# An attention and MoE kernel on one core: the fourth pair of the first group gets raw buffers of its own, GpSimd may round weights, VectorE no longer divides or copies for the early pairs

## Chip, cores, metric

One Trainium2 chip, one core. Times are device microseconds of that core for one execution of the whole program; smaller is better.

## What is computed

The reference is attention with a local window and a few global keys, and behind it a feed-forward layer (called MoE in the code; there is one expert):

```python
batch, n_heads, seq, head_dim = (4, 8, 768, 64)      # n_global 8, n_local 96
scores = scale * np.matmul(q, k.transpose(0, 1, 3, 2))
bias = -slopes[:, None, None] * dist[None, :, :]     # dist: |i - j|, n_local for global keys
scores = np.where(keep, scores + bias, -1000000000.0)
a = np.exp(scores - np.max(scores, axis=-1, keepdims=True))
a = a / (np.sum(a, axis=-1, keepdims=True) + 1e-09)
x = np.matmul(a, v)                                  # to [3072 tokens, 512]
h = x @ w_in                                         # 512 x 2048
g = np.where(h > 0.0, h, np.exp(np.minimum(h, 0.0)) - 1.0)
out = g @ w_out                                      # 2048 x 512
```

The weights come in as 64-bit floats and are turned into pairs of rounded 32-bit floats on the chip.

## The kernel before

**Tiling.** Tokens go in 12 groups of 256 (four batches, three groups each). Attention of a group is done in four pairs of heads, numbered hp 0 to 3; each pair has two tiles of 128 queries for two heads. A tile sees 232 keys (96 before it, 8 global ones, 128 of its own); the first tile of a batch sees 128. The two weight matrices are cut into 16 chunks of 128 hidden columns, fc 0 to 15. The first three groups go chunk by chunk (fc 0 to 4 for each of the three groups, then 5 to 9, then 10 to 15) with weights that are prepared meanwhile; from the fourth group on the MoE runs in a denser form (`moe7`), one fixed order for all groups.

**A pair of an early group** (`pair` and `pair32`, L482 and L677). Two loads bring it in: `rqv` (queries and values, L516, or L507 and L498 for the first three pairs) and `rk` (keys, L517 or L501). The queries are scaled (L528). TensorE makes the scores `s` (L691), VectorE adds the bias table and takes the maximum (`softmax`, L647), ScalarE takes the exponential with its sum (L649), VectorE adds 1e-9 and inverts the sums (L662, L663), and the four tiles `pr` are multiplied by the inverse: the division (`norm`, L671; helper `scaled`, L633 on ScalarE, L635 on VectorE, L637 on GpSimd). TensorE transposes (`t`, L708), the transposes are copied out of PSUM (`pt`, L715 and L718), TensorE multiplies with the values (`pv`, L725), and the result is rounded into `xh` (L533) with its remainder (L534). The helper `copy` is L336 on ScalarE and L338 on VectorE or GpSimd; `minus` is L344.

**A weight** (`weight`, L413). One load of 512 KB (`bits`, L425), then ScalarE's absolute value (L433), four steps of VectorE (L434, L438, L440, L442), the rounding to the high half (L444, run as L336) and the subtraction for the low half (L445, run as L344).

**The order.** The program is straight-line code, written in the order that a planner finds. Every operation is added with `p.add(alts, emit, reads, writes, due, ...)`. `alts` lists the engines that may do it, each with a planned duration and a mark for using the port that VectorE and GpSimd share (helpers `act`, `dve`, `pool`, L260 to L269). The planner takes operations as their inputs and buffers come free, by due time, and gives one with several engines to the engine on which it would end first. Each engine then runs its own list in order. All of these loads are issued by SyncE (SP) but one; its list is in order too, so a load that waits for a buffer holds up the loads behind it. Loads of early weights have the due time of their chunk less 9000: 21000 and 24500 for the first layer's chunks 0 and 1, 26800 and 30300 for the second layer's. Loads of raw pairs are due at the pair's time less 9000; for the fourth pair of the first group this is 11000.

**Buffers.** A tile class has named slots. Raw pairs of the first three groups have three slots each: `rqv0`, `w015`, `w115` for `rqv` and `rk0`, `w014`, `w114` for `rk` (the last two are weights' places that are not in use yet). `ks0` and `qs0` belong to later groups.

**After planning** (`run`, L1044) the loads of the chunks in `ASKED` (2, 3 and 4, both layers) are moved up in the list, to stand right behind the second group's second pair's load (`self.loads[10]`).

Of the kernel before, what the change touches and what calls it, by code (L numbers as in the profile page):

```python
# [16 lines left out]
P = 128  # L17
# [4 lines left out]
HK = WN // 2  # L22
NT = 2
W = NT * P
BIG = float(2 ** 100)

HI, LO = 0, 1
# [238 lines left out]


def pool(n, two=True):
    return (("POOL", (30 + 2.58 * n) if two else (50 + 1.1 * n), True),)  # L269


def sp():
# [3 lines left out]
class Kernel:  # L276
# [136 lines left out]
    def weight(self, which, fc, due, after):  # L413
# [21 lines left out]
        else:  # L435
# [5 lines left out]
              [bits, g], [g], due - 4500)  # L441
        p.add(dve(DM, port=True), lambda e: nc.vector.scalar_tensor_tensor(g.t, low(), 29, g.t, ALU.logical_shift_right, ALU.bitwise_or),  # L442
              [bits, g], [g], due - 4000)
        p.add(act(DM), lambda e: self.copy(e, w.t[:, HI], gf()), [g], [w], due - 3000)  # L444
        p.add((pool(DM) if due < 90000.0 else ()) + dve(DM, port=True), lambda e: self.minus(e, w.t[:, LO], gf(), w.t[:, HI]),  # L445
              [g, w], [w], due - 2000)
        if which == 0 or fc < self.NF7:
# [34 lines left out]
    def pair(self, b, gi, hp, xh, xl, due, ahead, step, X):  # L482
# [8 lines left out]
        rv = rqv if rows else self.sb("rv", "rv", [P, VC])  # L491
        rk = self.sb("rk", "rk", [P, nk], slots=X.get("rk"))
        src = self.qkv[b, gi, hp]
        early = due - 9000 if rows else ahead - 9000
        if b == gi == 0 and hp < 3:

            vs, ks = slice(nq + P, nq + VC), slice(k0, nk)
# [26 lines left out]
        if rows:  # L524

            if "held" in X:
                self.loads += loads
            p.add((() if b == gi == 0 and hp < 3 else act(W) + dve(W, True)) + pool(W, False),  # L528
                  lambda e: self.scaled(e, q32(), q32(), sc), [rqv], [rqv], due - 9000)
            pv = self.bank("pv", "pv", [P, NT, P], X.get("pv"))  # L530
            self.pair32(b, hp, t0, q32, k32, v32, rqv, rk, pv, due, step, X)
            pvs = lambda: pv.t.rearrange("p i w -> p (i w)")
            p.add(act(W, True) + dve(W), lambda e: self.copy(e, xh.t[:, HI, hp], pvs()), [pv], [xh], due + 700)  # L533
            p.add(dve(W), lambda e: self.minus(e, xh.t[:, LO, hp], pvs(), xh.t[:, HI, hp]), [pv, xh], [xl], due + 800)  # L534
            if "held" in X:
                self.held += [o for v in (rqv, rk) for o in v.readers]
            return
# [132 lines left out]

    def norm(self, pr, lo, st, i, due, both):  # L671
        n = WN - lo
        more = act(n, extra=90) + pool(n, False) if both else act(n)
        self.plan.add(more + (("DVE", 130 + 0.53 * n, True),), lambda e: self.scaled(
            e, pr.t[:, lo:], pr.t[:, lo:], st.t[:, 2, i:i + 1]), [pr, st], [pr], due)

    def pair32(self, b, hp, t0, q32, k32, v32, rqv, rk, pv, due, step, X):  # L677
# [22 lines left out]
        for j in range(2):  # L700
            for i, x in enumerate(tiles):
                self.norm(prs[j][i], x[2], st, j * NT + i, d - 3000 + 2 * j + i, True)
            tp = self.bank("t", "t", [P, NT, 2, P], X.get("t"))

            def transposes(e, j=j, tp=tp):
                for i, (_, _, _, a0, kr, blocks) in enumerate(tiles):
                    for a in range(a0, 2):
                        nc.tensor.transpose(tp.t[:kr, i, a], prs[j][i].t[:, blocks[a]], self.ident.t)  # L708

            n = sum(2 - x[3] for x in tiles)  # L710
            p.add((("PE", 20 + 108.0 * n, False),), transposes, prs[j], [tp], d - 2500 + j)
            pt = self.sb("pt", "pt", [P, NT, 2, P], slots=X.get("pt"))
            pts.append(pt)
            if t0:
                p.add(act(NT * 2 * P, True) + dve(NT * 2 * P), lambda e, pt=pt, tp=tp: self.copy(e, pt.t[:HK], tp.t[:HK]), [tp], [pt], d - 2000 + j)  # L715
            else:
                for i, (_, _, _, a0, kr, _) in enumerate(tiles):
                    p.add(act((2 - a0) * P, True) + dve((2 - a0) * P), lambda e, pt=pt, tp=tp, i=i, a0=a0, kr=kr: self.copy(  # L718
                        e, pt.t[:kr, i, a0:], tp.t[:kr, i, a0:]), [tp], [pt], d - 2000 + j)

        def values(e):
# [213 lines left out]
    def build(self):  # L935
# [25 lines left out]
        for n, (b, gi) in enumerate(groups):  # L961
            lo, hi = (0.0, self.T0) if n == 0 else (start[n - 1], start[n])
            lead = self.LEAD[n >= self.LATER]
            lo -= lead[0] if n else 0.0
            hi -= lead[1] if n else 0.0
            lo, hi = self.ATT.get(n, (lo, hi))
            st = (hi - lo) / (4 * self.NP)
            for hp in range(self.NP):
                d = lo + (hp + 1) * (hi - lo) / self.NP
                X_ = self.EARLY[min(n, len(self.EARLY) - 1)]  # L970
                if n > self.GS:
                    X_ = {"seven": True}
                ahead = last - 2500
                if n > self.GS:
                    ahead = start[self.GS] + self.PERIOD * (4 * (n - self.GS - 1) + hp - 2) + self.VISIT
                    d, st = ahead + self.AFTER, 600.0
                todo.append((d if X_.get("rows") else max(self.ATT[self.GS][1] + 1, last + 1 - 2 * self.PERIOD), lambda b=b, gi=gi, hp=hp, n=n, d=d, st=st, X_=X_, ahead=ahead: self.pair(
                    b, gi, hp, *X[n], d, ahead, st, X_)))
                last = d
# [36 lines left out]
    AFTER = 2 * PERIOD  # L1016
    PASSES, SINCE = 2, 195000.0
    GS, KEEP, COMBO = 3, 100000.0, 0.0
    LATE, ASKED = 11, (2, 3, 4)
    ABS = (0, 1)  # L1020
    LINE = 32
    PLACE = {"w015": (80, 0), "w014": (0, 48), "w012": (80, 0), "w013": (0, 48), "xh0": (160, 0), "xh1": (32, 0), "gg0": (80, 0), "gg1": (0, 0)}
# [293 lines left out]
```

## Time and profile before

| what | value |
|---|---|
| time, median of 3 runs | 654.95 us (654.11 to 655.26) |
| the profiled execution | 655.49 us, its span 653.7 us |
| TensorE busy | 642.0 us (98% of the span) |
| VectorE busy | 522.0 us (80%) |
| ScalarE busy | 478.4 us (73%) |
| GpSimd busy | 27.1 us (4%) |

The span runs from the first to the last instruction; the time has a little more around it. TensorE's records are pipelined and overlap, so that it can look busy while it is not at its full pace; the share of its weight loads (PEld) tells more. Shares over the whole span are a mean over stages: the tables by stage tell them apart.

### The profile page before, as it was taken

What the parts mean: (1) busy time and instruction counts of PE and PEld (TensorE: products, weight loads), DVE (VectorE), ACT (ScalarE), POOL (GpSimd) and SP (SyncE); (2) the same over time, 40 slices, a digit from 0 to 9 for tenths busy, and PEclk for the clock granted to TensorE, in tenths of its full rate; (3) what the DMA queues carried; (4) which work ended last, traced back from release to release, by engine and by line L of the source; (5) the groups of instructions that cost most, each with busy time, mean ns of one, the idle gap of its engine ahead of it and who ended that gap; (6) DMA issues with size and microseconds to landing.
All of it is one profiled execution on the core that took longest, in us unless ns stands there. A gap on an engine that the chain in (4) does not pass through costs nothing.

```text
span 653.7 us, 15985 instructions
## 1 busy us (share of the span) xinstructions
PE 642.0 (98%) x5950; PEld 599.4 (92%) x5950; DVE 522.0 (80%) x1520; ACT 478.4 (73%) x1244; POOL 27.1 (4%) x54
## 2 busy tenths in 40 slices
PE   8899999999999999999999999999999999999996
PEld 6677888888888999999999999999999999999996
DVE  7999999999999867866877886876777778766655
ACT  6898888765778777776777777776777777774442
POOL 3152100000000000000000000000000000000000
PEclk9999999999999999999999999999999999999999
DMA  8835996810237567667756756766775675574661
GB/s 273 293 118 193 383 379 223 301 61 17 71 114 255 198 212 255 224 196 224 264 187 214 272 180 221 253 218 202 230 262 181 223 282 189 178 255 169 209 211 36
DMA packets 52373, 137.71 MB, mean 211 GB/s; under 512 B 5698, under 2 KB 19010, under 8 KB 52290
## 3 DMA queue, kind: packets, MB, share of 16 engines
q1 hardware_dynamic: 52000, 136.37, 61.6%
q8 instruction: 48, 0.79, 0.5%
q14 instruction: 35, 0.29, 0.1%
q10 hardware_dynamic: 290, 0.26, 0.1%
HBM read 119.84 MB, written 16.78 MB: 209 GB/s over the span
## 4 chain that ended last, share of the span: by engine, by line
PE 90%; DVE 4%; ACT 2%; DMA 2%; issue 1%; POOL 0%; DVEq 0%; POOLq 0%; SPq 0%
PE h L803 39%; PE a L880 26%; PE o L763 9%; PE pv L614 4%; PE s L556 3%; PE t L576 3%; PE s L691 2%; DMA rqv<-in_qkv_dram 2%; PE pv L725 2%; PE t L708 2%; ACT pr L649 1%; DVE g L464 1%; PE none L1084 0%; DVE gl L344 0%; ACT pt L336 0%
## 5 line engine op out<-in xcount | busy, mean ns | idle before, releaser
L803 PE MATMUL h<-xh,w0s 128*128 128x256 f32 x1728 | 203.1, 276 | 0.0
L803 PEld LDWEIGHTS h<-xh,w0s 128*128 128x128 f32 x1728 | 199.5, 188 | 0.1
L880 PE MATMUL a<-w,gg 128*128 128x256 f32 x864 | 143.7, 277 | 0.3 <-DVE xh L344 0.3
L336 ACT CAST gg<-z 128x384 fp32r<-128x384 f32 (+1 forms) x144 | 81.4, 566 | 69.7 <-DVE z L735 29.7
L735 DVE SCALAR_TENSOR_TENSOR z<-z,h 128x512 f32<-128x512 f32 x72 | 49.5, 688 | 92.9 <-ACT z L734 86.0
L880 PEld LDWEIGHTS a<-w,gg 128*128 128x128 f32 x864 | 120.4, 188 | 0.6 <-DVE xh L344 0.5
L649 ACT ACTIVATE pr<-pr,nmax 128x232 f32<-128x232 f32 (+1 forms) x192 | 90.0, 471 | 9.2 <-DVE nmax L647 8.9
L344 DVE TENSOR_TENSOR gg<-z,gg 128x512 fp32r<-128x512 f32 (+1 forms) x144 | 84.9, 618 | 7.2 <-ACT gg L336 6.6
L803 PEld LDWEIGHTS h<-xh,w 128*128 128x128 f32 x576 | 81.7, 188 | 8.8 <-issue 1.1
L803 PE MATMUL h<-xh,w 128*128 128x256 f32 x576 | 86.7, 282 | 0.1
L835 DVE TENSOR_TENSOR z<-z 128x128 f32<-128x128 f32 (+1 forms) x216 | 72.0, 333 | 5.2
L880 PE MATMUL a<-ta,gg 128*128 128x256 f32 x432 | 72.2, 276 | 0.0
L647 DVE CUSTOM_DVE_ANT_0 pr<-s,tab 128x232 f32<-128x232 f32 (+1 forms) x192 | 63.5, 374 | 5.6 <-PE s L556 5.6
L733 ACT ACTIVATE z<-h 128x512 f32<-128x512 f32 x72 | 43.0, 597 | 33.2 <-PE h L803 32.9
L763 PE MATMUL o<-w,gh 128*128 128x512 f32 x192 | 59.8, 403 | 0.8 <-ACT gh L336 0.4
L880 PEld LDWEIGHTS a<-ta,gg 128*128 128x128 f32 x432 | 59.6, 188 | 0.0
L880 PE MATMUL a<-tb,gg 128*128 128x256 f32 x216 | 50.0, 294 | 0.0
L734 ACT ACTIVATE z<-z 128x512 f32<-128x512 f32 x72 | 45.5, 632 | 1.8
L633 ACT ACTIVATE pr<-pr,st 128x232 f32<-128x232 f32 (+1 forms) x90 | 38.9, 469 | 9.6 <-DVE st L669 7.3
L880 PEld LDWEIGHTS a<-tb,gg 128*128 128x128 f32 x216 | 34.4, 188 | 3.8 <-issue 0.2
L763 PEld LDWEIGHTS o<-w,gh 128*128 128x128 f32 x192 | 31.8, 188 | 5.8 <-ACT gh L336 1.1
L649 ACT ACTIVATION_READ_ACCUMULATOR pr<-pr,nmax 128x1 f32 x192 | 36.8, 192 | 0.0
(126 smaller groups left out, 916.4 us busy)
## 6 DMA issues: line engine op xcount, KB each, us to landing
w0s<-kept SPq DMA_DIRECT2D x144, 512.0 KB, 5.0
rk<-in_qkv_dram SPq DMA_DIRECT2D x45, 184.0 KB, 2.8
bits<-in_w_in_dram SPq DMA_DIRECT2D x16, 512.0 KB, 6.5
bits<-in_w_out_dram SPq DMA_DIRECT2D x16, 512.0 KB, 9.4
kept<-w SPq DMA_DIRECT2D x16, 512.0 KB, 4.4
rv<-in_qkv_dram SPq DMA_DIRECT2D x32, 256.0 KB, 3.6
rqv<-in_qkv_dram SPq DMA_DIRECT2D x13, 384.0 KB, 3.5
rqv<-in_qkv_dram SPq DMA_DIRECT2D x34, 128.0 KB, 3.8
```

What stands on the lines that cost most here:

```text
L336: self.nc.scalar.copy(out, x)
L344: self.on(e).tensor_tensor(out, x, y, ALU.subtract)
L633: self.nc.scalar.activation(out, x, AF.Copy, scale=sc)
L647: p.add((("DVE", 158 + 1.042 * n, False),), lambda e: nc.vector.tensor_tensor_reduce(pr.t[:, lo:], st_()[:, lo:], tab, -(2.0 ** -(h + 1)), ...
L649: p.add(act(n, extra=200), lambda e: nc.scalar.activation(pr.t[:, lo:], pr.t[:, lo:], AF.Exp, bias=nm, scale=-1.0, accum_out=st.t[:, 0, i: ...
L733: p.add(act(n, True), lambda e: nc.scalar.activation(out(), hx(), AF.Relu, scale=-1.0), [h], [ex], due)
L734: p.add(act(n), lambda e: nc.scalar.activation(out(), out(), AF.Exp, scale=-1.0), [ex], [ex], due)
L735: p.add(dve(n), lambda e: nc.vector.scalar_tensor_tensor(out(), out(), -1.0, hx(), ALU.add, ALU.max), [h, ex], [ex], due)
L763: nc.tensor.matmul(acc[i].t, g.t[:, i * P:(i + 1) * P], w2.t[:, s], start=fc == f0 and n == 0 and s == HI, stop=fc == f1 - 1 and n == 1)
L803: self.nc.tensor.matmul(hx(), w1.t[:, s, cc * P:(cc + 1) * P], xh.t[:, x, cc], start=n == 0 and cc == 0, stop=n == 2 and cc == self.NCC - 1)
L835: tt = lambda e, out, x, y, op: self.on(e).tensor_tensor(out, x, y, op)
L880: nc.tensor.matmul(of[i].t[:, j], gg.t[:, x, g], w(s), start=first and x == s == 0 and (n in (0, 2, 4, 6) or final and n == 5), stop=last ...
```

## The change

- The class of planned durations for GpSimd: one-input work is planned at 30 + 1.85 ns a column instead of 50 + 1.1 ns, and no longer marked as using the shared port. A new entry `cast` plans a rounding on GpSimd at 50 + 1.14 ns a column.
- The rounding of a weight's high half may run on ScalarE or GpSimd (before: ScalarE).
- The scaling of queries, the division of early pairs, the copies of transposes and the rounding of attention output lose VectorE as an alternative. Divisions and scalings stay with ScalarE or GpSimd, the two kinds that read PSUM with ScalarE.
- The fourth pair of the first group takes `ks0` for `rqv` and `qs0` for `rk`, and its loads are due at 25000 instead of 11000.
- `ASKED` holds chunk 2 alone.

```diff
 def pool(n, two=True):
-    return (("POOL", (30 + 2.58 * n) if two else (50 + 1.1 * n), True),)
+    return (("POOL", (30 + 2.58 * n) if two else (30 + 1.85 * n), two),)
+
+
+def cast(n):
+    return (("POOL", 50 + 1.14 * n, False),)
...
-        p.add(act(DM), lambda e: self.copy(e, w.t[:, HI], gf()), [g], [w], due - 3000)
+        p.add(act(DM) + cast(DM), lambda e: self.copy(e, w.t[:, HI], gf()), [g], [w], due - 3000)
...
-        early = due - 9000 if rows else ahead - 9000
+        early = X.get("asked", due - 9000) if rows else ahead - 9000
...
-            p.add((() if b == gi == 0 and hp < 3 else act(W) + dve(W, True)) + pool(W, False),
+            p.add((() if b == gi == 0 and hp < 3 else act(W)) + pool(W, False),
                   lambda e: self.scaled(e, q32(), q32(), sc), [rqv], [rqv], due - 9000)
...
-            p.add(act(W, True) + dve(W), lambda e: self.copy(e, xh.t[:, HI, hp], pvs()), [pv], [xh], due + 700)
+            p.add(act(W, True), lambda e: self.copy(e, xh.t[:, HI, hp], pvs()), [pv], [xh], due + 700)
...
-        more = act(n, extra=90) + pool(n, False) if both else act(n)
-        self.plan.add(more + (("DVE", 130 + 0.53 * n, True),), lambda e: self.scaled(
+        more = act(n, extra=90) + pool(n, False) if both else act(n) + (("DVE", 130 + 0.53 * n, True),)
+        self.plan.add(more, lambda e: self.scaled(
...
-                p.add(act(NT * 2 * P, True) + dve(NT * 2 * P), lambda e, pt=pt, tp=tp: self.copy(e, pt.t[:HK], tp.t[:HK]), [tp], [pt], d - 2000 + j)
+                p.add(act(NT * 2 * P, True), lambda e, pt=pt, tp=tp: self.copy(e, pt.t[:HK], tp.t[:HK]), [tp], [pt], d - 2000 + j)
...
-                    p.add(act((2 - a0) * P, True) + dve((2 - a0) * P), lambda e, pt=pt, tp=tp, i=i, a0=a0, kr=kr: self.copy(
+                    p.add(act((2 - a0) * P, True), lambda e, pt=pt, tp=tp, i=i, a0=a0, kr=kr: self.copy(
...
+                if n == 0 and hp == 3:
+                    X_ = dict(X_, rqv=["ks0"], rk=["qs0"], asked=25000.0)
...
-    LATE, ASKED = 11, (2, 3, 4)
+    LATE, ASKED = 11, (2,)
```

## Rows read from the trace of the kernel before

**Rows 1.** Engines by stage: stretch, its length, busy us (instructions) of PE, PEld, DVE, ACT, POOL, then clock, DMA.

```profile
5.00:60.00 55.00, 50.81 (x392) 38.76 (x389) 51.99 (x186) 48.82 (x156) 16.71 (x26) 1.00 0.63 213
60.00:201.00 141.00, 140.35 (x991) 122.33 (x992) 137.53 (x374) 108.74 (x297) 7.95 (x16) 1.00 0.55 200
```

**Rows 2.** The chain that ended last, 0 to 70 us: start, length, what.

```profile
19.52 4.09 DMA rqv<-in_qkv_dram
...
23.63 0.51 ACT rqv L633
...
34.02 0.73 PE o L763 x2
...
46.73 3.60 DMA rqv<-in_qkv_dram
...
59.28 0.60 POOL pr L637
```

**Rows 3.** TensorE in order of time: start, length, engine, line, operation, tiles, shape, count.

```profile
17.31 0.89 PE L691 MATMUL s<-rk,rqv 64*128 64x128 f32 x8
...
26.87 1.07 PE L803 MATMUL h<-xh,w 128*128 128x256 f32 x4
```

**Rows 4.** Loads: SyncE's issues in time; issue to landing and rates, 5.5 to 26 us.

```profile
5.08 0.43 SPq L425 DMA_DIRECT2D bits<-in_w_in_dram  x1
...
13.01 0.33 SPq L516 DMA_DIRECT2D rqv<-in_qkv_dram  x1
...
GB/s 349 403 422 346 342 318 330 384 440 392 416 416 442 367 370 376 322 214 327 180 24 0 0 90 156 414 154 175 155 131 137 398 344 344 308 200 224 296 376 360
...
bits<-in_w_in_dram SPq DMA_DIRECT2D x4, 512.0 KB, 5.7
rqv<-in_qkv_dram SPq DMA_DIRECT2D x3, 384.0 KB, 3.4
```

**Rows 5.** VectorE's groups, 5 to 60 us: count, busy us, mean ns, idle before.

```profile
L635 DVE TENSOR_SCALAR pr<-pr,st 128x232 f32<-128x232 f32 x8 | 3.0, 392 | 0.0
L635 DVE TENSOR_SCALAR rqv<-rqv,scale 128x256 f32<-128x256 f32 x5 | 2.5, 503 | 0.3 <-DMA rqv<-in_qkv_dram 0.3
...
L338 DVE CAST xh<-pv 128x256 fp32r<-128x256 f32 x3 | 1.2, 405 | 0.0
L338 DVE COPY pt<-t 116x256 f32<-116x256 f32 x2 | 0.8, 425 | 0.2 <-ACT pt L336 0.2
L338 DVE COPY pt<-t 116x512 f32<-116x512 f32 x1 | 0.7, 676 | 0.0
```

**Rows 6.** ScalarE's groups, 5 to 60 us, and one row of its timeline.

```profile
L336 ACT CAST w<-g 128x512 fp32r<-128x512 f32 x9 | 5.6, 618 | 0.0
...
L633 ACT ACTIVATE pr<-pr,st 128x232 f32<-128x232 f32 x11 | 5.2, 489 | 1.2 <-DVE st L663 1.2
...
L336 ACT COPY pt<-t 116x256 f32<-116x256 f32 x6 | 2.2, 373 | 0.0
...
L633 ACT ACTIVATE rqv<-rqv,scale 128x256 f32<-128x256 f32 x3 | 1.5, 509 | 1.0 <-DMA rqv<-in_qkv_dram 1.0
...
28.63 0.68 ACT L433 ACTIVATE g<-bits 128x512 f32<-128x512 f32 x1
```

**Rows 7.** GpSimd: a row of its timeline, and two groups of 5 to 60 us.

```profile
9.03 0.80 POOL L637 TENSOR_SCALAR pr<-pr,st 128x128 f32<-128x128 f32 x2 [2.60 <-ACT pr L649]
...
L344 POOL TENSOR_TENSOR w<-g,w 128x512 fp32r<-128x512 f32 x4 | 5.2, 1296 | 3.2 <-ACT w L336 3.0
...
L637 POOL TENSOR_SCALAR rqv<-rqv,scale 128x256 f32<-128x256 f32 x1 | 0.5, 481 | 1.0 <-DMA rqv<-in_qkv_dram 1.0
```

**Rows 8.** VectorE and GpSimd at the same time, from their timelines.

```profile
12.18 1.44 POOL L637 TENSOR_SCALAR pr<-pr,st 128x128 f32<-128x128 f32 x2 [2.35 <-DVE st L663]
...
52.75 1.27 POOL L344 TENSOR_TENSOR w<-g,w 128x512 fp32r<-128x512 f32 x1 [0.62 <-ACT w L336]
...
52.78 1.52 DVE L344 TENSOR_TENSOR gl<-e,gh 128x256 fp32r<-128x256 f32 x1
```

## Prediction

> **What bounds the kernel now.** I read the table of engines by stage first [rows 1]. From 60 to 201 us TensorE is busy 140.35 of 141 us, and its weight loads fill 122.33 us, 87% of the stage: the matmuls follow each other without a hole, so no other engine's work costs time there, and the steady part behind it goes on in the same way. From 5 to 60 us it is different. The weight loads fill only 38.76 of 55 us (70%). At the later stage's density that much loading would need 38.76 / 0.868 = 44.7 us, so 10.3 us are holes, and more in truth, because warm-up matmuls on the tile `none` count as work here. In that stage VectorE is busy 51.99 us (95%) and ScalarE 48.82 us (89%), but GpSimd 16.71 us (30%). What is saved before 60 us moves all later work forward; what is saved behind it is worth nearly nothing.
>
> Then the chain of waits inside that stage [rows 2]. It passes over TensorE in small pieces only. Between them stand a load of raw queries (19.52, 4.09 us), a stretch that is almost all ScalarE, from 23.63 to shortly before 34.02, and another load (46.73, 3.60 us); after that comes mostly VectorE, up to a division on GpSimd at 59.28. So three things end last in turn: loads of raw pairs, ScalarE, VectorE. The first MoE matmul starts at 26.87 [rows 3]; it needs the fourth pair of the first group, whose scores start at 17.31.
>
> **The change part by part.**
>
> *The fourth pair's buffers.* Now its queries are issued at 13.01, when the first pair has given its buffer back, and take about 3.4 us to land: 16.4 [rows 4]. With `ks0` and `qs0`, free until much later, its two loads are asked for at 25000. By the dues this lies behind the first layer's first two weights (21000 and 24500) and ahead of the second layer's two (26800 and 30300). So they go out behind the issue of 5.08. That weight takes about 5.7 us, landing at 10.8; the transfers run at some 390 GB/s there, so 568 KB more need 1.5 us: landed at about 12.3, 4 us sooner [rows 4]. The scores then stand behind the second pair's transposes in TensorE's queue, at 14 to 14.5 in place of 17.31: 3 us. The three older buffers go to the next group one step sooner, so the load of 19.52 no longer waits for the third pair's values, and its 4.09 us leave the chain. On SP two issues of 0.43 us are put before the second layer's first weights, which land 1.5 us later; the first matmul with them is at 34.02 [rows 2], so this costs nothing (1.5 us if that cover were gone). Weights 3 and 4 of both layers lose their place ahead in SP's queue: four loads of 512 KB go in their planned place, perhaps behind a load that waits for a buffer. ScalarE begins with weights 2 to 4 only at 28.63 [rows 6]: nothing again, with up to 3.6 us, a load's time as in [rows 2], if one comes late.
>
> *VectorE's divisions and copies.* Between 5 and 60 us VectorE loses 8 divisions (3.0 us), 5 scalings of queries (2.5), 3 roundings of attention output (1.2) and 3 copies of transposes (0.8 + 0.7): 8.2 us of its 51.99 [rows 5]. The roundings and copies read PSUM and go to ScalarE. There a copy of 256 columns takes 0.373 us [rows 6], and the one of 512 at most twice that: 5 x 0.373 + 0.75 = 2.6 us. The 13 divisions and scalings go to ScalarE or GpSimd, whichever is free first in the plan.
>
> *Weights' rounding.* ScalarE rounds 9 weights in that stage at 618 ns, 5.6 us [rows 6]; GpSimd may now take each. No row shows this on GpSimd. Its one-input operations take 0.40 us for 128 columns (two in 0.80) and 0.48 us for 256 [rows 7]; the line through these gives 0.64 us for 512. The lower end is the 0.48 us of half the size, the upper the two-input subtraction of 512 columns, 1.30 us. I take 0.7, near the one-input rows. Below ScalarE's 0.62 it would be a small gain in latency, no more.
>
> *The planner's figures.* One-input work on GpSimd is planned longer (504 ns for 256 columns; the row has 481) and no longer closes the shared port to VectorE in the plan. By itself this costs nothing, but the order of all that follows is planned anew. That can add or take away some tenths of a us; I take 0.
>
> *The sum.* VectorE's 13 divisions and scalings and ScalarE's 14 (11 + 3) can now all go to GpSimd. GpSimd is idle 70% of the time, ScalarE 11%, so I give GpSimd two thirds of these 27 and of the 9 roundings. ScalarE: 48.8 + 2.6 - 6 x 0.618 - (14 - 9) x 0.489 = 45.3 us. VectorE: 52.0 - 8.2 + 1 for waiting at the port = 44.8 us. GpSimd: 16.7 + 6 x 0.7 + 18 x 0.5 = 29.9 us. ScalarE is now the longer one by a hair. Filled as now (88.8%), its work takes 45.3 / 0.888 = 51.0 us of the 55: 4.0 us less. Filled as VectorE is now (94.5%), 47.9 us: 7.1 us less. If GpSimd takes only a third (3 roundings, 9 of the 27), ScalarE has 48.8 + 2.6 - 1.9 + 4 x 0.489 = 51.5 us, and nothing is won. I take 4.0 us, the filling that the rows show for this engine. The earlier loads are not added to that: they are what keeps ScalarE filled when its work gets shorter (it waits 1.0 us for a load now [rows 6]). The profiled execution took 655.49 us, 0.5 us over the median of the runs shown, 654.95. 655.49 - 4.0 = 651.5; against the median **651.0 us**.
>
> **The port that VectorE and GpSimd share.** The trace shows the two holding each other up: a subtraction on VectorE at 52.78 took 1.52 us while GpSimd subtracted from 52.75 to 54.02 [rows 8]; another operation of that size takes 0.41 [rows 5]. Two of GpSimd's divisions took 1.44 us at 12.18 [rows 8], two others 0.80 [rows 7]. The Trainium skill has this as a rule (SBUF — State Buffer, "Who interferes with whom"): the pair of ports is an exclusive lock for a whole instruction, and a VectorE instruction with two SBUF inputs, or in a two-port mode, contends with GpSimd's reads. These rows agree with it. The rule speaks against this change: if each of the 24 added GpSimd operations held such an instruction for its length, some 24 x 0.55 = 13 us would come back on VectorE, where the sum has 1 us.
>
> **Rivals.**
>
> *GpSimd becomes the late one (slower).* A pair's transposes wait for all four of its divisions; already the chain runs over a division on GpSimd of 0.60 us at 59.28 [rows 2]. With roundings of 0.7 us in the same queue, a division can stand behind one, and be locked out as well (0.72 us each in place of 0.40, rows above). It decides from the point where this falls on most of the eight pairs of groups two and three: 8 x (0.7 + 0.32) = 8.2 us, against some 6 us that the rest saves, so 2 us slower: 657 us. For it: that chain, and the collisions. Against: GpSimd is idle 70%, and the planner picks the engine that ends first. Chance 0.17.
>
> *ScalarE takes VectorE's place (no change).* The sum's lower end: ScalarE gets the copies, GpSimd few roundings, and the stretch from 23.63 on only moves. The loads bring the 1.0 us that ScalarE waits: 654 us. For it: ScalarE alone holds that stretch. Against: GpSimd has room, and the planner compares ends. Chance 0.17, of which 0.05 are faster by over 0.2%.
>
> *Everything closes up.* The filling rises to 94.5% and the first MoE matmul comes at about 22: 7.1 us less, 647.9 us. Chance 0.14.
>
> *The buffers do nothing*, because TensorE's queue keeps the fourth pair's scores where they are. Then the engines' gain counts from 27 us on alone: 4.0 x 33 / 55 = 2.4 us, 652.6 us, at the forecast's edge. It has 0.10 of the forecast's chance.
>
> **How the numbers follow.** Forecast 0.52 (own range 649 to 653), everything closes up 0.14, ScalarE in place 0.17, GpSimd late 0.17. A measurement of this kernel can tell about 0.2% (1.3 us) from no change. Faster by over 0.2%: 0.52 + 0.14 + 0.05 less 0.02 at the forecast's edge = 0.69; within 0.14 (0.12 + 0.02); slower 0.17. The range leaves out the far halves of the fast and the slow case: 647.2 to 656.5.
>
> **What would show it.** Right: the first MoE matmul before 24 us; no load of raw queries in the chain near 20 us; VectorE at 80 to 90% and GpSimd at 45 to 60% between 5 and 55 us; TensorE dense some 4 us sooner, and all behind it moved by the same. Wrong: ScalarE at 95% or more from 20 to 55 us (the second rival); transposes waiting for GpSimd's divisions, and long subtractions on VectorE like the one of 52.78 (the first); new holes behind 60 us would say that the new order, not the early stage, decides.

## The result, and the profile after

The changed kernel takes **662.60 us** (median of 5 runs, 661.84 to 664.19) against 654.95 (654.11 to 655.26): a ratio of 1.012, 95% interval 1.0108 to 1.0131, 7.6 us slower. The forecast was 651.0, and the range ended at 656.5. Two executions among all the later runs, of 1049.27 and 1267.45 us, stand far apart from the others of their kernels and are in no median and no ratio below. The change adds four lines ahead of most of the code, so L803 of before is L807 of after.

By stage, as in [rows 1] (stretch, its length, busy us and instructions of PE, PEld, DVE, ACT, POOL, then clock, DMA share, GB/s):

```profile
5.00:60.00 55.00, 47.21 (x380) 35.93 (x379) 48.05 (x166) 47.08 (x157) 31.31 (x43) 1.00 0.58 202
60.00:201.00 141.00, 140.27 (x984) 121.91 (x983) 133.79 (x356) 106.79 (x295) 24.68 (x32) 1.00 0.56 204
```

The work moved the way that the sum said: VectorE fell from 51.99 to 48.05 us, ScalarE from 48.82 to 47.08, and GpSimd rose from 16.71 to 31.31. TensorE got nothing of it. Its weight loads fill 35.93 us of the first stage, where [rows 1] have 38.76. Three rows of TensorE in time, as in [rows 3] (the idle time ahead in brackets):

```profile
12.42 0.89 PE L695 MATMUL s<-rk,rqv 64*128 64x128 f32 x8 [1.92 <-POOL rqv L641]
18.48 1.05 PE L695 MATMUL s<-rk,rqv 64*128 64x232 f32 x8 [1.81 <-POOL rqv L641]
28.45 0.72 PE L807 MATMUL h<-xh,w 128*128 128x256 f32 x4
```

The fourth pair's scores run at 12.42 in place of 17.31, but the first MoE matmul comes at 28.45 in place of 26.87. The chain of waits, 0 to 75 us, as in [rows 2]:

```profile
11.84 0.49 POOL rqv L641
12.42 0.89 PE s L695 x8
...
17.95 0.49 POOL rqv L641
18.48 1.05 PE s L695 x8
...
22.67 1.77 POOL pr L641 x2
...
28.19 1.46 DVE g L444 x2
29.64 0.34 DVE xh L348
29.98 1.20 DVE g L446 x2
...
36.61 1.20 DVE g L444 x2
...
38.15 1.29 DVE g L446 x2
...
41.06 1.17 POOL pr L641 x2
...
43.47 0.91 POOL rqv L641
...
46.59 4.87 DMA rqv<-in_qkv_dram
51.62 0.62 POOL rqv L641
```

The load of 19.52 has left the chain, and so has the stretch of ScalarE. In their place stand GpSimd's scalings of queries, each with scores behind it, GpSimd's divisions, and from 27 to 41 us almost nothing but VectorE, mostly with the preparation of weights (`g`). Between 5 and 60 us the chain passes over VectorE for 18.2 us, where it did for 8.8 before: the engine that the change relieves is waited for longer than it was.

In this execution all that costs little. The steady part (the first matmul `h<-xh,w0s`) starts at 202.4 us, where it started at 201.4: 1.0 of the 7.6 us. The rest is lost behind, where TensorE has no hole in either kernel: from that start to the end of the span it is 452.3 us before and 458.4 after. First the kernel before, then the one after: the chain of waits between 240 and 320 us (48 matmuls of one chunk pair), and the group of these matmuls over the whole execution (busy us, mean ns):

```profile
252.84 5.44 PE h L803 x48
...
303.55 5.65 PE h L803 x48
...
L803 PE MATMUL h<-xh,w0s 128*128 128x256 f32 x1728 | 203.1, 276 | 0.0
```

```profile
253.88 5.74 PE h L807 x48
...
306.01 5.44 PE h L807 x48
...
L807 PE MATMUL h<-xh,w0s 128*128 128x256 f32 x1728 | 207.7, 279 | 0.0
```

The same 48 matmuls take 5.44 us (113.3 ns each) in before and 5.74 us (119.6 ns) in after, in every second group of rows. Both have a granted clock of 1.00 there. Summed, `h` with `w0s` is 4.6 us longer, and the second layer's matmuls (`a`) 1.3.

What differs is not in the diff. The pool `m` lays out its slots in the order of their first use, and the new plan has another order. Two things moved. `ks0` and `qs0` are used at the start, so they now lie ahead of nearly everything: `xh0` goes from byte 174368 to 179488 of each partition, 5120 bytes or 40 times 128. And `gg0`, which lay behind `xh1`, now has its first use ahead of it: `gg0` goes from 192928 to 189728, and `xh1`, with the 7488 bytes of `gg0` now before it, from 184608 to 197216. That is 12608 bytes, 64 more than a multiple of 128. The ring of weights stays. The slow groups are those whose moving operand lies in `xh1`.

### The profile page after: what moved, and what is told of

The parts are those of the page before. It is cut to its first block, busy times and chain, and to the rows that moved or that the text cites. A ratio compares the mean times of both kernels' runs of the same rounds, so it can differ in the third digit from the quotient of the medians.

```text
span 660.8 us, 15992 instructions
## 1 busy us (share of the span) xinstructions
PE 645.4 (98%) x5941; PEld 603.2 (91%) x5941; DVE 515.1 (78%) x1490; ACT 474.2 (72%) x1242; POOL 58.4 (9%) x86
## 4 chain that ended last, share of the span: by engine, by line
PE 83%; DVE 11%; issue 2%; ACT 1%; DMA 1%; POOL 1%; SPq 0%; POOLq 0%; DVEq 0%
PE h L807 36%; PE a L884 27%; PE o L767 6%; PE pv L618 4%; PE s L560 4%; PE t L580 3%; DVE g L444 2%; DVE g L446 1%; PE pv L729 1%; PE t L712 1%; DVE w L348 1%; PE s L695 1%; DVE e L739 1%; DVE gl L348 1%; DVE g L438 1%
## 5 line engine op out<-in xcount | busy, mean ns | idle before, releaser
L807 PE MATMUL h<-xh,w0s 128*128 128x256 f32 x1728 | 207.7, 279 | 0.0
L807 PEld LDWEIGHTS h<-xh,w0s 128*128 128x128 f32 x1728 | 204.0, 189 | 0.1
L807 PEld LDWEIGHTS h<-xh,w 128*128 128x128 f32 x576 | 82.5, 188 | 9.7 <-issue 2.3
L807 PE MATMUL h<-xh,w 128*128 128x256 f32 x576 | 88.4, 283 | 0.6 <-DVE e L739 0.6
L637 ACT ACTIVATE pr<-pr,st 128x232 f32<-128x232 f32 (+1 forms) x94 | 40.8, 471 | 9.3 <-DVE st L673 7.2
L340 ACT COPY pt<-t 128x128 f32<-128x128 f32 (+2 forms) x88 | 37.4, 438 | 2.8 <-PE t L712 1.5
```

Source lines behind the costliest of these rows:

```text
L340: self.nc.scalar.copy(out, x)
L637: self.nc.scalar.activation(out, x, AF.Copy, scale=sc)
L807: self.nc.tensor.matmul(hx(), w1.t[:, s, cc * P:(cc + 1) * P], xh.t[:, x, cc], start=n == 0 and cc == 0, stop=n == 2 and cc == self.NCC - 1)
```

## The experiments

### Places in SBUF: the steady part

Two runs exchange the layouts and nothing else. Empty tiles in the wanted order are taken ahead of the first instruction:

```
+            for s in "w015 w014 ... rqv0 rk0 pr0 pr1 st0 ... ks0 part0 part1 vd0".split():
+                (self.w if s[0] == "w" else self.m).tile([P, self.LINE], F32, tag=s, name=self.n("place"))
             free = self.plan.FREE["PE"]
```

> The changed kernel, with each of its buffers put where the kernel before has it in SBUF (the pool hands out addresses in the order of first use; empty tiles in the old order are taken ahead of the first instruction). Nothing else differs. Placement theory: the 5.7 us that the changed kernel loses behind 202 us come from xh1 and gg0 having moved, so the spacing of the h matmuls falls from 120 to 113 ns wherever it was 120, the steady part starts at 202.4 us as in the changed kernel and the whole takes 656.0 us (655.5 to 656.7). Rival, the new order of instructions: the steady part runs as in the changed kernel whatever the addresses, and the whole takes 662 us (661 to 663).

> The kernel before, with each buffer put where the changed kernel has it. Nothing else differs. Placement theory: the first 201 us are those of the kernel before, the h matmuls of every second group then take 120 ns in place of 113, and the whole takes 660.6 us (659.5 to 661.5). Rival, the new order: 655 us (654.3 to 655.7).

With the new places the kernel before takes **660.72 us** (ratio 1.0083, 1.0070 to 1.0096): 5.7 us lost, as the placement theory said (660.6), and its rival (655) falls. With the old places the changed kernel takes **657.32 us** (ratio 1.0030, 1.0017 to 1.0044), 5.3 us less than as given; expected were 656.0, and the range given for it ended at 656.7. The rows show the exchange: the kernel before with the new places, then the changed kernel with the old ones.

```profile
253.00 5.74 PE h L803 x48
...
L803 PE MATMUL h<-xh,w0s 128*128 128x256 f32 x1728 | 207.4, 279 | 0.0
```

```profile
259.64 5.44 PE h L807 x48
...
L807 PE MATMUL h<-xh,w0s 128*128 128x256 f32 x1728 | 203.4, 277 | 0.0
```

The profiled run of the changed kernel with the old places is the slowest of its 12 (662.87 us, mean granted clock 0.99), so that its steady part starts late, at 208.3. From that start to the end of the span it is 452.8 us long; in the kernel before with the new places (start at 201.5) it is 458.1. So the addresses cost 5.3 to 5.7 us, and the order of instructions costs at most some 0.5 us in the steady part. The runs of changed kernels below have the old places, but for the next.

The next sets only offsets inside four slots:

```
-    PLACE = {..., "xh0": (160, 0), "xh1": (32, 0), "gg0": (80, 0), "gg1": (0, 0)}
+    PLACE = {..., "xh0": (32, 0), "xh1": (48, 0), "gg0": (112, 0), "gg1": (80, 0)}
```

> The changed kernel, its buffers in the new order, with only the offsets inside four slots of SBUF set anew (xh0 32, xh1 48, gg0 112, gg1 80 elements in place of 160, 32, 80, 0), so that xh0 and xh1 again begin at 416 bytes and gg0 and gg1 at 224 bytes past a multiple of 512, as in the kernel before; xh1 still lies 12 KB higher than there. Phase theory: it is the position within 512 bytes that sets the spacing of the h and a matmuls, so all of them are back at 113 ns and the whole takes 656 to 657.5 us, as the changed kernel with the old places did. Rival, the place itself (its distance or region): xh1 keeps its 120 ns and the whole takes 661.5 to 663 us.

It takes **665.20 us** (ratio 1.0149, 1.0132 to 1.0167). Both theories miss. No stretch of `h` is at 120 ns any more, `xh1` included, which speaks for the position. But many stretches, of both `xh0` and `xh1`, are now at 117.8 ns, as in the second row here, and only some at 113.3:

```profile
255.93 5.44 PE h L807 x48
267.74 5.65 PE h L807 x48
```

To take everything else away I measured the spacing by itself:

> The computation is left out: one tile of SBUF is filled with ones, then 64 stretches of 48 matmuls of the h form (256 columns moving, 128x128 stationary, fp32r) run back to back with nothing else active, each with its own byte addresses of the moving tile and of the stationary tile. Stretches 1 to 8: the addresses of xh and of the four slots of weights as in the kernel before (175008, 184736), the changed kernel (180128, 197344) and the changed kernel with the old phases (179616, 197024), then 197344 and 184736 again. Stretches 9 to 24 and, backwards, 25 to 40: moving tile from 184320 in steps of 32 bytes, stationary at 4832. Stretches 41 to 56: moving at 184736, stationary from 4608 in steps of 32. 57 to 64: both moved on together by 64. Theory, the addresses alone set the spacing: 5.76 us (120 ns) in the stretches at 197344 and 5.44 us (113.3 ns) in those at 184736, 175008 and 180128, and in the sweep slow positions that come again when it is run backwards. Rival, the spacing needs the other engines' traffic to the same SBUF: 5.44 us in all 64.

The addresses alone give the 120 ns. The stretches, cut at their first matmuls, with TensorE's busy time (a stretch holds 48; the count has a neighbour at each edge). The first four rows take the stationary tiles of the kernels' ring in turn: `xh0` of after, 180128; `xh1` of after, 197344; `xh1` with the old phase, 197024; 197344 again. The last two have one stationary tile, at 4832: 184608 on the way up, and the same pair of addresses on the way back.

```profile
37.55:42.99 5.44, 5.44 (x50) 5.44 (x49) 0.00 (x0) 0.00 (x0) 1.00 0.00 0
42.99:48.73 5.74, 5.74 (x50) 5.74 (x49) 0.00 (x0) 0.00 (x0) 1.00 0.00 0
54.20:59.63 5.43, 5.43 (x50) 5.43 (x49) 0.00 (x0) 0.00 (x0) 1.00 0.00 0
59.63:65.38 5.75, 5.75 (x51) 5.75 (x50) 0.00 (x0) 0.00 (x0) 1.00 0.01 3
121.97:127.63 5.66, 5.66 (x50) 5.66 (x49) 0.00 (x0) 0.00 (x0) 1.00 0.01 3
196.10:201.54 5.44, 5.44 (x50) 5.44 (x49) 0.00 (x0) 0.00 (x0) 1.00 0.01 3
```

From the matmuls' starts (the first stretch aside, which ran up slowly): in the stretches with the ring's tiles the spacing is 113.3 to 113.7 ns where the moving tile's address is 64 bytes past the stationary one's, counted modulo 128, and 119.6 where it is 0 past it. In before, `xh0` and `xh1` lie 64 past the ring's tiles; in after, `xh1` lies 0 past them, and that comes from `gg0` being laid out ahead of it. The room of `ks0` and `qs0` alone, 5120 bytes, keeps the 64, and `xh0`, moved by it alone, stays at 113.3 (180128, the first row). That is worked out from the places; no run moves one slot by itself.

With one stationary tile the picture is less clean. At a difference of 64 only two of twelve stretches are at 113.4 and ten at 117.8 to 117.9; at the other differences tried (0, 32, 96) the spacing lies between 116.7 and 120.0, and where both are moved together at difference 0 it is 119.7 to 119.8 in all eight stretches. The last two rows show that one pair of addresses has two spacings, in two places of the sequence with other stretches ahead. So a difference of 64 was needed for the 113 ns in this run, but it is not enough. The 117.8 ns are also the spacing of the slow stretches in the run with the old phases, and of 303.55 in before; what puts a pair into the slower of the two stays open.

The Trainium skill (SBUF — State Buffer, "Who interferes with whom") gives TensorE two read ports, one for the moving operand and one for the weight load, and calls them independent; only the ports that VectorE and GpSimd share would contend. By that, the position of the two operands relative to each other shouldn't matter. In this run it does, by up to 6% with no other engine active; in which part of TensorE the time goes isn't shown.

### The two halves of the change

> Of the change only the fourth pair's own raw buffers and its earlier load (asked 25, only the third of the early weights is put ahead); costs and choices of engines as before; every buffer where the kernel before has it. If the early load gains what the prediction allowed it (the 4.09 us that the chain spends on the raw load at 19.5 us, less what is late next), the first MoE matmul comes 1.5 to 3 us before 26.9 and the whole takes 652 to 653.5 us. Rival, the load was hidden or its place in the queue costs others as much: 654.5 to 656 us.

> Of the change only the new choice of engines (GpSimd takes part in the rounding of the weights, VectorE makes no divisions or copies, GpSimd's price for one input); loads and buffers as before; every buffer where the kernel before has it. Theory of the late GpSimd: each scaling or division that GpSimd now makes on the way to the next matmul is later by 0.4 to 1.9 us, some of it in the open, so the steady part starts 1 to 3 us behind 201.4 and the whole takes 656 to 658 us. Rival, as predicted, VectorE's and ScalarE's relief counts: 651.5 to 653.5 us.

The buffers alone take **659.23 us** (ratio 1.0050, 1.0030 to 1.0071), the engines alone **660.54** (1.0070, 1.0056 to 1.0084). Both missed both their theories, on the slow side. Together they take 657.32, less than either half: the halves don't add, and neither gains anything when it stands alone. Part of their loss is the clock: six of the seven runs with the buffers alone and all six with the engines alone have a mean granted clock below 0.998, and the one above it (buffers, 657.02) is 2.0 us behind the kernel before. In the profiled run with the buffers alone (the slowest, 662.94, at a clock of 0.83 to 0.86 up to 27 us) the first MoE matmul comes at 29.28, and the load of the next raw pair is in the chain once more, issued at 23.57 and 5.47 us long where [rows 2] have 4.09.

Three more leave out a piece of the engines' half. Port planned: GpSimd's one-input operations are planned as holding the port.

```
-    return (("POOL", (30 + 2.58 * n) if two else (30 + 1.85 * n), two),)
+    return (("POOL", (30 + 2.58 * n) if two else (30 + 1.85 * n), True),)
...
-    return (("POOL", 50 + 1.14 * n, False),)
+    return (("POOL", 50 + 1.14 * n, True),)
```

VectorE back: the five alternatives `dve(...)` that the diff takes away are put back. No shared rounding: `act(DM) + cast(DM)` is `act(DM)` again.

> The changed kernel with the old places, and the planner told that GpSimd's operations with one input (scalings, divisions, the rounding) can't run beside VectorE's operations that hold the shared port, as it was told before the change; prices as in the change. Theory of the lock-out: GpSimd's lateness comes from operations placed beside such VectorE work (divisions of 1.77 to 2.6 us in place of 0.48), so planned apart they cost less; the steady part starts at 199 to 201 us in place of 202.4, and the whole takes 653.5 to 655.5 us. Rival, the lateness is GpSimd's own time and its queue: 656 to 658 us as without this edit.

> The changed kernel with the old places, and VectorE allowed again to make divisions, scalings and copies where it is free first; buffers, earlier load and the shared rounding as in the change. If taking VectorE away is what made the early stage late (the matmuls wait for GpSimd's scalings 1.92, 1.81 and 1.66 us at 12.4, 18.5 and 52.3), the steady part starts 1 to 3 us ahead of 202.4 and the whole takes 653.5 to 655.5 us. Rival, the early loads set the early stage whatever the engines do: 656 to 659 us, as with the buffers alone.

> The changed kernel with the old places, the rounding of the weights left to ScalarE alone as before; the rest as in the change. If the roundings on GpSimd (0.60 us alone, up to 1.76 beside VectorE) hold up its scalings, the whole is 0.5 to 2 us faster than with them, 655 to 656.5 us. Rival, they are relief for ScalarE, as predicted: 658 to 660 us without them.

They take **657.65** (ratio 1.0031, 1.0017 to 1.0045), **659.95** (1.0071, 1.0054 to 1.0088) and **657.76 us** (1.0046, 1.0029 to 1.0063) beside 657.32 with all of it. Planning for the port (as its rival said) and leaving out the rounding (outside both its theories) change nothing that these runs can tell; giving VectorE back makes it worse, outside both its theories. So neither the rounding nor VectorE's missing share is by itself what ate the gain.

### TensorE's clock, and the fourth pair's place in the queue

With the old places the runs of the changed kernel spread from 655.57 to 662.87. The six with a mean granted clock of 0.998 or more have a median of 656.2, the six below that 658.9. The profiled one, the slowest, by stage (columns as above):

```profile
5.00:16.00 11.00, 8.69 (x48) 6.30 (x46) 6.94 (x36) 7.82 (x30) 4.01 (x8) 0.88 0.96 352
16.00:27.00 11.00, 9.99 (x68) 6.91 (x64) 8.29 (x30) 8.90 (x34) 5.40 (x8) 0.81 0.58 187
```

The granted clock is 0.88 and 0.81 of full speed, a mean of the two levels (2.4 and 1.2 GHz), with TensorE busy 8.69 of 11 us in the first of them and waiting ahead of scores, as at 12.42 and 18.48 in after. Such waits were there in the kernel before, but shorter: 1.7 us in all between 5 and 60 us, the longest in the row below, and 6.4 us in after.

```profile
20.79 1.05 PE L691 MATMUL s<-rk,rqv 64*128 64x232 f32 x8 [1.35 <-ACT rqv L633]
```

Ahead of scores the kernel issues no filler. One run fills these waits, one puts the fourth pair's loads ahead of the first weights (`asked=9000.0`), one does both (with `asked=14000.0`; TensorE, GpSimd and SyncE have the same order in both runs):

```
-                    if op.allocs[0].cls != "s":
-                        self.warm(min(op.start - free, 1150.0), 300.0)
+                    self.warm(min(op.start - free, 1150.0), 300.0)
```

> The changed kernel with the old places, and the filler matmuls that keep TensorE busy in planned gaps are issued ahead of score matmuls too, ahead of which the kernel has none. Theory of the clock: the changed order makes TensorE wait ahead of score matmuls (12.4, 18.5 us), unfilled, and in some executions the granted clock then falls to half for some microseconds (0.81 to 0.88 in 5 to 27 us of the run with the old places); filled, the clock stays at 0.998 to 1.0 and the whole takes 656.2 us, all within 655.5 to 657. Rival, the clock isn't it, or the filler stands in the way: 657 us and more, as wide as without (655.6 to 662.9).

> The changed kernel with the old places, the fourth pair's raw loads ahead of the first weights in the DMA queue and not behind them. Theory, the fourth pair's load now ends the wait of the first scores behind 9 us (landed at 11.8 to 13.1, scores at 12.4 to 13.8): it lands by 9 us, the scores run some 2 to 3 us sooner, the first weights land 1.2 us later, the whole is 0.5 to 2 us faster, 655 to 656.5 us. Rival, the first weights are late next: the same or slower, 657 to 659 us.

> Both of the last two edits: fourth pair's raw loads ahead of the first weights, filler ahead of score matmuls. If both theories hold 654.5 to 656 us, the best of the changed kernels and about the kernel before (655.0); if neither, 657 to 659 us.

Filled, the clock holds in all 12 runs (0.998 to 1.0), and the profiled one shows it:

```profile
5.00:16.00 11.00, 10.95 (x64) 6.77 (x62) 7.66 (x38) 7.76 (x30) 2.87 (x7) 1.00 0.97 358
16.00:27.00 11.00, 9.53 (x70) 6.50 (x69) 10.07 (x37) 10.03 (x39) 9.03 (x13) 1.00 0.81 254
```

The time is **656.70 us** (1.0023, 1.0011 to 1.0035). The clock is as its theory said; of the time, 0.6 us of the 1.1 that it gave (656.2) came in the median, and three of the 12 runs are above its 657. With the loads first it is **656.05** (1.0014, 1.0003 to 1.0025), inside what its theory gave, with the scores at 8.82 in the profiled run. But ten of these 12 runs have a clock of 0.998 or more, and among such runs it is 655.9 against 656.2: most of the gain in the median is the clock. With both it is **657.49** (1.0037, 1.0020 to 1.0054), as if neither theory held: again no adding up, and in 6 of its 12 runs the clock is at 0.997 or less although the gaps are filled. Why is open.

### What the engines' time is worth, with the order held

The last question is the sum itself. Three runs keep the order of instructions and shorten operations that are planned in the first 60 us to 2 columns. The run on VectorE has the first edit below, the run on GpSimd the second, and the run on all three has both, with `e != "DVE"` as the condition:

```
+        few = lambda x: x[:, :2] if self.now < 60000.0 else x
...
-            p.add(dve(DM, True), lambda e: nc.vector.tensor_scalar(gf(), gf(), F64_MIN, F64_MAX, ALU.max, ALU.min), [g], [g], due - 5500)
+            p.add(dve(DM, True), lambda e: nc.vector.tensor_scalar(few(gf()), few(gf()), F64_MIN, F64_MAX, ALU.max, ALU.min), [g], [g], due - 5500)
...
     def scaled(self, e, out, x, sc):
+        if e == "POOL" and self.now < 60000.0:
+            out, x = out[:, :2], x[:, :2]
```

> The kernel before, its order of instructions unchanged; of the computation, the clamping of the first weights (planned in the first 60 us) is left out but for 2 of 512 columns. In 5 to 60 us this takes 10 operations of 432 ns from VectorE down to bare ones of some 0.1 us, 3 us or more. If the busy time of the three engines sets the early stage, as the prediction summed it, 3.2 us over three engines and 0.888 is 1.2 us: 653.8 us. If VectorE alone is the bound, 3 us: 652 us. If the early stage hangs on landings and on the order, less than 0.5 us: 654.6 to 655.2 us.

> The kernel before, its order unchanged; of the computation, the clamping as in the run with less VectorE work, and the scalings and divisions of ScalarE and GpSimd planned in the first 60 us are left out but for 2 columns. In 5 to 60 us VectorE loses some 3 us, ScalarE 14 operations of 0.49 to 0.51 us down to some 0.25 (3.5 us), GpSimd 20 or more of 0.47 to 0.55 us. If busy time is the bound, (3 + 3.5 + 4) / 3 / 0.888 = 4 us and the whole takes 651 us; if landings and the order are, 653.5 to 655 us.

> The changed kernel with the old places, its order unchanged; of the computation, GpSimd's scalings and divisions planned in the first 60 us are left out but for 2 of 232 or 256 columns (28 operations of 0.55 to 0.72 us there). Theory of the late GpSimd: the matmuls' waits for them (4.5 us ahead of the scores in 5 to 60 us) shrink to under half, the steady part starts 2 us or more sooner, 653.5 to 654.5 us at full clock. Rival, other waits come to their place (landings, VectorE's softmax): less than 1 us, 655.5 to 656.5 us.

VectorE's ten clamps went from 432 to 178 ns, 2.5 us less; the time is **654.40 us** (ratio 0.9988, 0.9979 to 0.9997), 0.2 to 1.4 us less, between what busy time (653.8) and what landings and order (654.6 and more) would give: VectorE alone is not the bound. With all three relieved (2.7 us of VectorE, 2.9 of ScalarE, about 4.7 of GpSimd) it is **652.77** (0.9966, 0.9952 to 0.9980), 1.3 to 3.1 us less, again between its two theories (651, and 653.5 and more). The prediction's rule, ScalarE's time over 0.888, gives 2.9 / 0.888 = 3.3 for that. So the rule is on the high side but not far off, as long as the order stands; which of the three engines gave the gain isn't taken apart.

In the changed kernel the shortened scalings and divisions bring the median from 657.32 to **654.11** (0.9988 of the kernel before, 0.9973 to 1.0003). In runs with a clock of 0.998 or more it is 653.3 in place of 656.2: 2.9 us. So the late GpSimd is shown; its theory's range (653.5 to 654.5) lay a little too high. The scores' waits for scalings, 4.8 us in the profiled run with the old places, are 1.0 us, with 2.1 us for a load of keys beside them. The groups of GpSimd's divisions, 5 to 60 us: the kernel before; the changed kernel; the changed kernel with 2 columns; the kernel before with 2 columns.

```profile
L637 POOL TENSOR_SCALAR pr<-pr,st 128x232 f32<-128x232 f32 x13 | 7.1, 553 | 21.3 <-DVE st L663 17.4 <-ACT w L336 4.0
```

```profile
L641 POOL TENSOR_SCALAR pr<-pr,st 128x232 f32<-128x232 f32 x16 | 11.4, 722 | 4.9 <-DVE st L667 3.1 <-ACT xh L340 1.3 <-ACT pr L653 0.5
...
L695 PE MATMUL s<-rk,rqv 64*128 64x232 f32 x72 | 11.1, 413 | 4.5 <-POOL rqv L641 4.5
...
L342 POOL CAST w<-g 128x512 fp32r<-128x512 f32 x9 | 6.7, 755 | 6.5 <-DVE g L446 4.9 <-ACT g L437 1.6
```

```profile
L643 POOL TENSOR_SCALAR pr<-pr,st 128x2 f32<-128x2 f32 x21 | 11.2, 547 | 8.2 <-ACT pr L655 6.0 <-ACT xh L340 1.6 <-DVE st L669 0.4
```

```profile
L640 POOL TENSOR_SCALAR pr<-pr,st 128x2 f32<-128x2 f32 x20 | 6.0, 314 | 32.8 <-DVE st L666 13.0 <-ACT w L336 12.2 <-ACT xh L336 5.3
```

The same two columns take 314 ns in the order of before and 547 in the order of after. The 233 ns between them are no work. The timeline of the changed kernel with 2 columns shows what they are: of two divisions in a row, the first runs beside a VectorE operation that reads PSUM (`pv`), the second beside one with all its operands in SBUF.

```profile
21.11 0.42 DVE L348 TENSOR_TENSOR xh<-pv,xh 128x256 fp32r<-128x256 f32 x1
...
21.15 0.27 POOL L643 TENSOR_SCALAR pr<-pr,st 128x2 f32<-128x2 f32 x1 [0.32 <-ACT xh L340]
...
21.39 0.80 POOL L643 TENSOR_SCALAR pr<-pr,st 128x2 f32<-128x2 f32 x1
21.46 0.68 DVE L446 SCALAR_TENSOR_TENSOR g<-bits,g 128x512 int32<-128x512 int32 x1
```

All 21 follow this. Eight have nothing of VectorE beside them, or only operations that read PSUM (`xh<-pv,xh`, `pr<-s,tab`) and the short read-outs behind these: they take 262 to 270 ns. Thirteen have an operation on SBUF alone beside them (`g<-bits,g`, `g<-g`, `w<-g,w`, `gl<-e,gh`): 442 to 1224 ns. So GpSimd's divisions grow by standing beside VectorE's preparation of weights, at the port that the two share. That this by itself cost the time is not shown: planned apart, 8 of GpSimd's 21 divisions have such an operation beside them where 12 of 20 had one, and the time stayed (657.65 and 657.32). And the 4.5 us that 72 score matmuls wait are all put down to GpSimd's scalings.

### Can a complete kernel have it?

Three complete kernels joined what came nearest. The first has the fourth pair's loads first and the port planned; the other two have the loads first and take the queries' scalings off GpSimd from the fourth pair on, the last with the port planned too:

```
-            p.add((() if b == gi == 0 and hp < 3 else act(W)) + pool(W, False),
+            p.add(pool(W, False) if b == gi == 0 and hp < 3 else act(W) + dve(W, True),
```

> The changed kernel with the old places, complete: the fourth pair's raw loads ahead of the first weights, and the planner told that GpSimd's operations with one input hold the shared port. If the gains of the two edits add up (1.2 and 0.5 us at full clock on 656.2) 654.5 to 655.5 us, as the kernel before or a little faster; if each new order is a draw of its own, anywhere in 655 to 659 us.

> The changed kernel with the old places, complete: fourth pair's loads ahead of the first weights, and the scalings of raw queries, for which the score matmuls wait, given to ScalarE or VectorE from the fourth pair on (divisions and roundings stay with GpSimd and ScalarE). The run with GpSimd's work shortened gave 2.9 us at full clock. If most of that was the scalings', 653.5 to 655 us, faster than the kernel before; if it was the divisions' or VectorE is late in turn, 655.5 to 657 us.

> As the kernel above, and the planner told that GpSimd's operations with one input hold the shared port. If the edits that came nearest add up, 653 to 654.5 us; if each new order is a draw of its own, 654.5 to 657 us, on either side of the kernel above.

They take **655.17** (ratio 0.9998, 0.9986 to 1.0010), **658.48** (1.0055, 1.0036 to 1.0074) and **657.60 us** (1.0040, 1.0025 to 1.0054). The first is as the kernel before; that fits both its theories. The other two are slower than either of theirs: moving the scalings elsewhere doesn't bring what leaving them out brought. No complete version here beats the kernel before. Twelve of them with the old places, in ten orders, lie between 655.2 and 660.5 us, and small edits moved them by up to some 3 us in no direction that I could foretell.

## Why the prediction was wrong, point by point

Two steps failed, and each is about half of the 11.6 us between 651.0 and 662.60.

- **"the steady part behind it goes on in the same way"**: this step failed, and it is 5.3 to 5.7 us, most of the 7.6 us that the change lost. The argument was that no other engine can cost time where TensorE has no hole. That left out that TensorE's own pace could change. The step on the buffers counted who waits for `ks0` and `qs0` and when they are free; the step on the new order took it at 0. Neither asked in which order the slots are first used and so laid out, and it is that order, with `gg0` ahead of `xh1`, that shifts `xh1` by 64 modulo 128. The offsets of `PLACE`, set slot by slot, stood in the code to be asked about.
- **The sum of 4.0 us**: this step failed as well. With the old places the changed kernel stands 1.2 us behind the kernel before at full clock and 2.3 in the median (657.32), outside the range even without the addresses. First, the engines lost less work than said: ScalarE has 47.08 us where 45.3 was said, VectorE 48.05 for 44.8 (GpSimd 31.31 for 29.9). By the prediction's own rule, 47.08 / 0.888 = 53.0 us of the 55, that is 2.0 us less and not 4.0. GpSimd took nearly all the roundings and scalings, but 21 divisions where it had 20; its time grew also because they got longer. Second, the rule prices an engine's busy time, and the added work was waited for result by result: scores wait 6.4 us where they waited 1.7, and the chain passes over VectorE for 18.2 us where it did for 8.8. The sum had no term for that. Shortening GpSimd's scalings and divisions gave back 2.9 us at full clock, which says what they cost in this order; the same was not run on the kernel before by itself, and these effects overlap, so that they don't divide the 5.2 us between -4.0 and +1.2. The clock adds 1.1 in the median.
- **The 1 us of waiting at the port**: too small, and on one engine alone. VectorE's ten clamps went from 432 to 547 ns, its ten shifts from 423 to 477 and its longest two-input operations from 681 to 725: 2.1 us in these three groups. In after, clamps and shifts that begin with no GpSimd operation under way take 396 to 428 ns; of the fourteen that begin under one, eight take 577 to 835. GpSimd's divisions went from 553 to 722 ns, and the sum had added GpSimd work at 0.5 us each. The two groups of clamps, before and after:

```profile
L434 DVE TENSOR_SCALAR g<-g 128x512 f32<-128x512 f32 x10 | 4.3, 432 | 0.3 <-ACT g L433 0.3
```

```profile
L438 DVE TENSOR_SCALAR g<-g 128x512 f32<-128x512 f32 x10 | 5.4, 547 | 0.6 <-ACT g L437 0.6
```

- **Rounding on GpSimd, 0.7 us**: 0.755 measured, 9 of them: right. Leaving it out changed nothing that the runs can tell.
- **"GpSimd becomes the late one"**, rival with a chance of 0.17, 2 us slower: its place was right but for one thing. It named the divisions ahead of the transposes (0.8 us of waiting in after); the longest waits were scores behind scalings (6.4 us). Its price for a division that is locked out, 0.72 us, is near the means that were measured (652 ns at 128 columns, 722 at 232). It was held unlikely because GpSimd is idle 70%. How idle an engine is doesn't tell whether what it does is waited for.
- **The fourth pair's loads**: they landed about when I said (11.76 against 12.3) and the scores came 5 us sooner, 3 said; the load of 19.52 left the chain. The first MoE matmul came later all the same (28.45, where 22 to 24 was said).
- **The new order, taken at 0**: the complete versions with the old places lie up to 5.4 us apart, by new orders and by the small changes of work that made them; a price of this size belonged into the range. And the new order is what laid `gg0` ahead of `xh1`.

## What to carry to other kernels

A change of buffers or of their first use is also a change of addresses: compare the layout before and after, and the pace of the same matmuls in a stage that the change doesn't touch, before any wait is looked at. Work moved to an idle engine is priced by who waits for each single result, and by the port that the engine shares, not by its idle share. Where an order comes out of a planner, hold the order and shorten one operation to learn what its time is worth, since any edit of the costs draws a new order, and the ten orders here lie up to 5.4 us apart, more than the 4.0 us that were sought.

## What the runs showed of the hardware

Matmuls of 256 fp32r columns with no other engine active followed each other at 113.3 to 113.7 ns where the moving tile lay 64 bytes past the stationary tiles of the ring modulo 128, and at 119.6 ns where it lay 0 past them, at a granted clock of 1.00 in both. With one stationary tile, the same pair of addresses ran at 113.4 and at 117.9 ns in two places of the run. A division of two columns on GpSimd took 262 to 270 ns beside no VectorE operation or one that reads PSUM, and 442 to 1224 ns beside one on SBUF alone.
